# A Fourier mixing layer and a tanh-shrink feed-forward layer on one core: another order of the element-wise steps, of the transforms' banks and of the second layer's products

## The chip, the cores and the metric

The kernel runs on one core of a Trainium2 chip. A core has a matrix engine (TensorE, PE in the profile), two engines for element-wise work that can read the matrix engine's output memory (VectorE, DVE, and ScalarE, ACT), a third for element-wise work[...] (GpSimd, POOL), and DMA queues. Each engine works through its own instructions in the order in which the program lists them, and engines wait for each other at semaphores. Matmul results go to PSUM[...]; a bank here is one tile of 128 partitions by 512 fp32 values.

The metric is the time of one execution on the device, in microseconds.

## The reference

```python
# x (8, 3008, 256), filters (1505, 256), w_in (256, 2048), w_out (2048, 256), all fp32
X = np.fft.rfft(x, axis=1)
Y = X * (filt_r + 1j * filt_i)[None]
y = np.fft.irfft(Y, n=3008, axis=1)
tokens = y.reshape(8 * 3008, 256)
h = tokens @ w_in
g = h - np.tanh(h)
out = g @ w_out
```

The length 3008 is split as 64 times 47. The transform is a chain of small matmuls with data laid out again through device memory in between: `first` (its results `pf`), then `middle` (a forward product `pz`, the filter, a backward product `pe`), then `last` (`pu`, which gives the tokens of one group). The batch is worked off in five units of one or two sequences: while the feed-forward layer of one unit runs, the transforms of the next are put between its matmuls, one at a time.

Both layers of the feed-forward part use a scheme in which a two-by-two block product takes seven block products instead of eight, numbered 1 to 7. Their weights and sums of weights are made at the start; the sums of the other operand are made as the kernel goes (`tu` for the tokens, `t` for the hidden values). `h - tanh(h)` is computed as h times y times a polynomial in y, with y the square of an arctangent of scaled h.

## The kernel before

The loop runs over U, from 0 to 193. A step U holds three things at different depths: `up(U)`, the first layer of 512 of the 2048 hidden columns for a group of up to 512 tokens; `shrink(U - 1)`, the element-wise function of the step before; `down(U - 2)`, its second layer. Four U (u = 0 to 3) make one group. `up` is the frame, and calls the next piece of `shrink` (`s`), the next piece of `down` (`d` and `e`) and a possible transform (`t(0)` to `t(4)`) at fixed places:

```python
    def up(U, d, e, s, t):
        i, u = divmod(U, 4)
        b, tu, w = uts[i]
        rhs = [b[0][0], b[1][0], b[1][1], tu[:, 3, 0:w], tu[:, 0, 0:w], tu[:, 1, 0:w],
               tu[:, 2, 0:w]]
        banks = {k: ps.tile([128, 2, 256], F32, tag=k, bufs=1, name=k) for k in "xyz"}
        X, Y, Z = (banks[k][:, :, 0:w] for k in "xyz")
        h = dn.tile([128, 4, 2, 256], F32, tag="h", bufs=3, name="h")
        hs[U] = (h, w)
        def mm(bank, q, first):
            for k in range(2):
                nc.tensor.matmul(bank[:, k], wu[:, q - 1, (2 * u + k) * 128:(2 * u + k + 1) * 128],
                                 rhs[q - 1], start=(first and k == 0), stop=True,
                                 skip_group_check=True)
        def copied(tag):
            t = dn.tile([128, 2, 256], F32, tag=tag, bufs=1, name=tag)[:, :, 0:w]
            ACT.copy(t, X)
            return t
        steps_at = ([1, 2, 0, 1, 0, 1, 1, 0] if U > 1 else [0, 0, 1, 0, 2, 0, 1, 2])
        def shrinks(at):
            for _ in range(steps_at[at]):
                s()
        mm(X, 1, True)
        mm(Y, 2, True)
        s1 = copied("s1")
        t(0)
        d()
        shrinks(0)
        V.tensor_add(h[:, 0, :, 0:w], Y, s1)
        e()
        shrinks(1)
        t(1)
        mm(X, 6, False)
        mm(Z, 5, True)
        u2 = copied("u2")
        shrinks(2)
        d()
        shrinks(3)
        e()
        t(2)
        mm(X, 7, False)
        u3 = copied("u3")
        V.tensor_add(h[:, 3, :, 0:w], Z, u3)
        shrinks(4)
        d()
        shrinks(5)
        e()
        t(3)
        mm(X, 4, False)
        V.tensor_copy(h[:, 2, :, 0:w], X)
        shrinks(6)
        d()
        e()
        t(4)
        mm(Z, 3, False)
        V.tensor_add(h[:, 1, :, 0:w], Z, u2)
        shrinks(7)
    def shrink(U):
        h, w = hs.pop(U)
        ht = {k: h[:, k:k + 2].rearrange("p a b n -> p (a b) n")[:, :, 0:w] for k in (0, 2)}

```

X, Y and Z are three PSUM banks with one tile each. X and Z take several products one after another: they are read out in between, and the next product adds to what is there. `h[:, 0]` to `h[:, 3]` are the four blocks of hidden values.

The element-wise function of a step comes in six pieces; half 2 is h2 and h3, half 0 is h0 and h1. `combine` makes the four sums of blocks on GpSimd:

```python
        yield
    def combine(b, t, shared=False):
        G.tensor_sub(t[0], b[0][1], b[0][0])
        G.tensor_sub(t[1], b[1][1], t[0])
        (V if shared else G).tensor_sub(t[2], b[1][1], b[0][1])
# ...
            return dn.tile([128, 4, 256], F32, tag=tag, bufs=bufs, name=tag)[:, :, 0:w]
        y, sq = {}, {}
        def start(k):
            y[k] = tiles("y", 2)
            ACT.activation(y[k], ht[k], AF.Arctan, scale=S)
            ACT.activation(y[k], y[k], AF.Square,
                           accum_out=y_sums[:, 2 * U + k // 2:2 * U + k // 2 + 1])
        def square(k):
            sq[k] = tiles("sq", 1)
            V.tensor_mul(ht[k], ht[k], y[k])
            ACT.activation(sq[k], y[k], AF.Square, bias=near_b, scale=A)
        def end(k):
            V.scalar_tensor_tensor(out=ht[k], in0=sq[k], scalar=K, in1=ht[k],
                                   op0=ALU.add, op1=ALU.mult)
        start(2)
        yield
        square(2)
        yield
        end(2)
        yield
        start(0)
        yield
        square(0)
        yield
        end(0)
        t = dn.tile([128, 4, 2, 256], F32, tag="t", bufs=2, name="t")
        blocks = [[h[:, 2 * a + k, :, 0:w] for k in range(2)] for a in range(2)]
        combine(blocks, [t[:, k, :, 0:w] for k in range(4)], U + 1 == 4 * len(groups))
        gs[U] = (blocks, t, w)
        yield
    accs, stores, outs = {}, [], []
```

The second layer has eight pieces, called in turn by `d` and `e`. Seven sums stay in four banks over the four U of a group:

```python

        i, u = divmod(U, 4)
        b, t, w = gs.pop(U)
        rhs = [b[0][0], b[1][0], b[1][1], t[:, 3, :, 0:w], t[:, 0, :, 0:w], t[:, 1, :, 0:w],
               t[:, 2, :, 0:w]]
        if u == 0:
            accs[i] = [ps.tile([128, 2, 256], F32, tag=f"o{k}", bufs=1, name=f"o{k}")
                       for k in range(4)]
        acc = accs[i]
        at = {1: (0, 0), 2: (0, 1), 3: (1, 0), 5: (1, 1), 6: (2, 0), 7: (2, 1), 4: (3, 0)}
        def product(q):
            bank, k = at[q]
            return acc[bank][:, k, 0:w]
        def mm(*qs):
            for k in range(2):
                for q in qs:
                    nc.tensor.matmul(product(q), wd[:, q - 1, (2 * u + k) * 128:
                                                    (2 * u + k + 1) * 128],
                                     rhs[q - 1][:, k], start=(u == 0 and k == 0 and q == qs[0]),
                                     stop=(u == 3 and k == 1), skip_group_check=True)
        done = u == 3
        if done:
            p1, p5, u2, x12 = (dn.tile([128, 256], F32, tag=k, bufs=1, name=k)[:, 0:w]
                               for k in ("p1", "p5", "pu2", "x12"))
            o = dn.tile([128, 2, CH * 128], F32, tag="o", bufs=1, name="o")
        mm(1, 2)
        yield
        if done:
            ACT.copy(p1, product(1))
            V.tensor_add(o[:, 0, 0:w], product(2), p1)
        yield
        mm(3, 5)
        yield
        if done:
            ACT.copy(p5, product(5))
            V.tensor_add(x12, product(3), p5)
        yield
        mm(6, 7)
        yield
        if done:
            V.tensor_add(u2, product(6), p1)
            V.tensor_add(p1, product(7), u2)
            G.tensor_add(o[:, 0, w:2 * w], u2, x12)
        yield
        mm(4)
        yield
        if done:
            V.tensor_add(o[:, 1, 0:w], product(4), p1)
            G.tensor_add(o[:, 1, w:2 * w], p1, p5)
            accs.pop(i)
            if i + 1 < len(groups):
                stores.append((i, o))
            else:
                store_last(i, o)
        yield
    def store(i, o):

```

A transform asks for a bank with `zd`; `quarter` is the place, 0 to 4, at which `t` was called, and `latest` the bank of the last transform. There are two banks for it, t (its own) and y (the same bank as Y above):

```python
            quarter, latest = [1], ["t"]
            def zd(name, shape):
                latest[0] = "y" if quarter[0] in (1, 2, 3) and latest[0] == "t" else "t"
                return ps.tile(shape, F32, tag=latest[0], bufs=1, name=name)
```

One step of `middle` is a `pz` with its filter, the next one a `pe` of the `pz` before:

```python
        def back():
            j, uv = waiting.pop(0)
            pe = z("pe", [128, per, w])
            for i in range(per):
                k = per * j + i
                nc.tensor.matmul(pe[0:RP2, i], mats[k // 4][1][:, k % 4], uv[0:IM + RP, i],
                                 start=True, stop=True)
            e1 = tr.tile([RP2, 2, DM], F32, tag="e1", bufs=2, name="e1")
# ...
            pz = z("pz", [128, per, w])
            at, ft = a2[j // 2] if j % 2 == 0 else a2.pop(j // 2)
            for i in range(per):
                k = per * j + i
                lo = j % 2 * BD + i * w
                nc.tensor.matmul(pz[:, i], mats[k // 4][0][0:R2, k % 4],
                                 at[0:R2, lo:lo + w], start=True, stop=True)
            uv = tr.tile([128, per, w], F32, tag="uv", bufs=2, name="uv")
            zs = tr.tile([128, per, w], F32, tag="zs", bufs=2, name="zs")
            lo = j % 2 * per
            fr, fi = (ft[:, v, lo:lo + per, :] for v in range(2))
            if pair:
                fr, fi = (f.to_broadcast([128, 2, DM]) for f in (fr, fi))
            def rows(t):
                return t.rearrange("p i (b c) -> p (i b) c", c=DM)
            ACT.mul(zs[0:IM], pz[IM:128], -1.0)
            ACT.copy(zs[IM:128], pz[0:IM])
            V.tensor_mul(rows(uv), rows(pz), fr)
            G.tensor_mul(rows(zs), rows(zs), fi)
            G.tensor_add(uv, uv, zs)
            waiting.append((j, uv))
            yield
            if len(waiting) > 1:
                back()
                yield
        back()
```

Which transform is called, if any, follows from the step's number: at quarters 0 and 2 of u = 3 it is always a `pu`; elsewhere the pieces of `first` and then of `middle` are spread over the unit's steps.

Of the kernel before, what the change touches and what calls it, by code (L numbers as in the profile page):

```python
# [9 lines left out]
F32 = mybir.dt.float32  # L10
# [133 lines left out]
def kernel(  # L144
# [10 lines left out]
    V, G, ACT = nc.vector, nc.gpsimd, nc.scalar  # L155
# [376 lines left out]
    def up(U, d, e, s, t):  # L532

        i, u = divmod(U, 4)
        b, tu, w = uts[i]
        rhs = [b[0][0], b[1][0], b[1][1], tu[:, 3, 0:w], tu[:, 0, 0:w], tu[:, 1, 0:w],
               tu[:, 2, 0:w]]
        banks = {k: ps.tile([128, 2, 256], F32, tag=k, bufs=1, name=k) for k in "xyz"}
        X, Y, Z = (banks[k][:, :, 0:w] for k in "xyz")
        h = dn.tile([128, 4, 2, 256], F32, tag="h", bufs=3, name="h")  # L540
        hs[U] = (h, w)

# [11 lines that stand above are left out]

        steps_at = ([1, 2, 0, 1, 0, 1, 1, 0] if U > 1 else [0, 0, 1, 0, 2, 0, 1, 2])

        def shrinks(at):
            for _ in range(steps_at[at]):  # L560
# [10 lines that stand above are left out]
        shrinks(1)  # L571
        t(1)
        mm(X, 6, False)
        mm(Z, 5, True)
        u2 = copied("u2")
        shrinks(2)
# [8 lines that stand above are left out]
        d()  # L585
        shrinks(5)
        e()
        t(3)
        mm(X, 4, False)
        V.tensor_copy(h[:, 2, :, 0:w], X)  # L590
        shrinks(6)
        d()
        e()
# [10 lines that stand above are left out]
        def tiles(tag, bufs):  # L604
            return dn.tile([128, 4, 256], F32, tag=tag, bufs=bufs, name=tag)[:, :, 0:w]

        y, sq = {}, {}

        def start(k):
            y[k] = tiles("y", 2)  # L610
            ACT.activation(y[k], ht[k], AF.Arctan, scale=S)  # L611
            ACT.activation(y[k], y[k], AF.Square,  # L612
                           accum_out=y_sums[:, 2 * U + k // 2:2 * U + k // 2 + 1])

        def square(k):
            sq[k] = tiles("sq", 1)
            V.tensor_mul(ht[k], ht[k], y[k])  # L617
            ACT.activation(sq[k], y[k], AF.Square, bias=near_b, scale=A)  # L618

        def end(k):  # L620
            V.scalar_tensor_tensor(out=ht[k], in0=sq[k], scalar=K, in1=ht[k],  # L621
                                   op0=ALU.add, op1=ALU.mult)

        start(2)
        yield
        square(2)
        yield
        end(2)
        yield
        start(0)  # L630
        yield
        square(0)
        yield
        end(0)
        t = dn.tile([128, 4, 2, 256], F32, tag="t", bufs=2, name="t")
        blocks = [[h[:, 2 * a + k, :, 0:w] for k in range(2)] for a in range(2)]
# [3 lines that stand above are left out]
# [3 lines left out]
    def down(U):  # L643
# [18 lines that stand above are left out]
                for q in qs:  # L662
                    nc.tensor.matmul(product(q), wd[:, q - 1, (2 * u + k) * 128:  # L663
                                                    (2 * u + k + 1) * 128],
                                     rhs[q - 1][:, k], start=(u == 0 and k == 0 and q == qs[0]),
                                     stop=(u == 3 and k == 1), skip_group_check=True)

        done = u == 3
        if done:
            p1, p5, u2, x12 = (dn.tile([128, 256], F32, tag=k, bufs=1, name=k)[:, 0:w]  # L670
                               for k in ("p1", "p5", "pu2", "x12"))
            o = dn.tile([128, 2, CH * 128], F32, tag="o", bufs=1, name="o")
        mm(1, 2)
        yield
        if done:
            ACT.copy(p1, product(1))
            V.tensor_add(o[:, 0, 0:w], product(2), p1)
        yield
        mm(3, 5)
        yield  # L680
        if done:
            ACT.copy(p5, product(5))
            V.tensor_add(x12, product(3), p5)
        yield
# [18 lines that stand above are left out]
# [136 lines left out]
    with tc.tile_pool(name="tr", bufs=2) as tr, tc.manual_schedule():  # L839
        with tc.tile_pool(name="pro", bufs=1) as pro, \  # L840
                tc.tile_pool(name="ps0", bufs=6, space=bass.MemoryType.PSUM) as ps0:

            def z0(name, shape):
                return ps0.tile(shape, F32, tag="z", bufs=6, name=name)
# [132 lines left out]
            for j in range(NK // 2):  # L977
# [6 lines left out]
                pz = z0("pz", [128, 2, DM])  # L984
                for i in range(2):
                    k = (2 * j + i) % 4
# [34 lines left out]
        with tc.tile_pool(name="dn", bufs=2) as dn, \  # L1021
                tc.tile_pool(name="ps", bufs=1, space=bass.MemoryType.PSUM) as ps:

            quarter, latest = [1], ["t"]

            def zd(name, shape):
                latest[0] = "y" if quarter[0] in (1, 2, 3) and latest[0] == "t" else "t"
                return ps.tile(shape, F32, tag=latest[0], bufs=1, name=name)  # L1030

            psums.append(zd)
# [37 lines left out]
            for U in range(total + 2):  # L1070
                i, u = divmod(U, 4)
                if U < total:
                    p, c = groups[i]
                    if c == 0 and u == 0:
                        units = 4 * len(CHUNKS[p])
                        steps, done = [], 0 if p else EARLY
# [21 lines left out]
                def d():  # L1098

                    next(dw, None)  # L1100

                def e():

                    next(dw, None)

                def s():

                    next(sh, None)

                def t(k):  # L1110


                    nonlocal ms, done
                    quarter[0] = k
                    if k == 2 and stores:
                        store(*stores.pop())
                    store_some(4)
                    if U >= total:
                        return
                    pos = 20 * c + 5 * u + k  # L1120
                    if u == 3 and k in (0, 2) and i + 1 < len(groups):
                        next(lasts)
                    elif done < len(steps) and steps[done] <= pos:
                        if done < n_f:
                            next(fs)
                        else:
                            next(ms)
                        done += 1
                        if done == n_f:
                            ms = middle(p + 1, z1)  # L1130
                            next(ms)
                    next(late, None)
                    if U > 0 and k in (1, 3):
                        next(copies, None)
# [56 lines left out]
```

## Time and profile before

| What | Value |
|---|---|
| Time, median of 3 runs | 2817.25 us (2815.6 to 2819.74) |
| Span of the profiled execution | 2817.1 us |
| TensorE busy | 2725.6 us, 12438 matmul instructions |
| VectorE busy | 1913.8 us |
| ScalarE busy | 1877.0 us |
| GpSimd busy | 1796.2 us |
| DMA | 217.53 MB, 77 GB/s in the mean |

A row of the profile's groups names the line, the engine, the operation and the tiles (out<-in), the number of instructions, their busy time and the mean duration of one in ns. A row of the waits reads: engine, tile and line that waited, whom it waited for, microseconds in total, number of times, longest. A row of the timeline reads: start in us, duration in us, engine, line, operation, tiles, number of instructions merged into it, and in brackets the idle time before it with its releaser. PE is a matmul, PEld a weight load. Recorded ends of matmuls lie behind the start of the next one, since they are pipelined. One matmul of the program is two matmul instructions in the trace, so a group of two calls on 256 columns shows as x4.

Lines of the kernel before: L545 first layer, L551 copies out of X, L569, L583, L590 and L596 the VectorE readings of Y, Z, X and Z that give h0, h3, h2 and h1; L611 arctangent, L612 its square, L618 square with bias, L617 product, L621 end of the element-wise function; L524 to L527 the sums on GpSimd; L663 second layer; L430, L411, L351 and L511 `pz`, `pe`, `pf` and `pu`; L443 and L444 ScalarE's two readings of `pz`, L445 VectorE's, L446 and L447 GpSimd's part of the filter.

### The profile page before, as it was taken

Reading aid. Unit: us, or ns where it says so; the run is one execution under the profiler, and the core shown is the slowest. Engines: PE = TensorE matmul, PEld = TensorE weight load, DVE = VectorE, ACT = ScalarE, POOL = GpSimd, SP = SyncE. Lnnn points to the kernel's source line nnn. Section 1 sums busy time; section 2 is a strip of 40 time slices with the busy share of each in tenths; the row PEclk is TensorE's granted clock in tenths of the full one; section 3 lists DMA queues with packets and bytes.
Section 4 is the critical chain, followed back from the end, with each engine's and each line's share of the span. In section 5 each row is a group of like instructions: output and inputs, shape, how many; then the busy total and the mean of one; then the engine's idle time right before and its main releaser. Section 6 shows DMA issues by size and latency. Waiting matters only on the chain.

```text
span 2817.1 us, 36653 instructions
## 1 busy us (share of the span) xinstructions
PE 2725.6 (97%) x12438; PEld 2268.1 (81%) x12438; DVE 1913.8 (68%) x2175; ACT 1877.0 (67%) x2790; POOL 1796.2 (64%) x1407
## 2 busy tenths in 40 slices
PE   4899999999999999999999999999999999999998
PEld 2577777888878777888878887888888888898887
DVE  6755666666766676666677767666676777677776
ACT  2466776666667766666667776666666676666665
POOL 5546887544776767644576777755476666655555
PEclk7999999999999999999999999999999999999999
DMA  9854443332333322223323233112223322101010
GB/s 248 220 180 118 104 123 76 87 87 72 72 77 79 74 68 61 58 81 83 88 70 76 68 79 81 40 41 67 58 65 64 77 56 57 30 19 26 16 23 17
DMA packets 322592, 217.53 MB, mean 77 GB/s; under 512 B 224782, under 2 KB 274746, under 8 KB 322156
## 3 DMA queue, kind: packets, MB, share of 16 engines
q1 hardware_dynamic: 266826, 157.28, 24.0%
q10 hardware_dynamic: 52818, 51.53, 6.0%
q0 software_dynamic: 2752, 6.30, 0.8%
q8 instruction: 100, 1.64, 0.3%
q14 instruction: 96, 0.79, 0.1%
HBM read 138.87 MB, written 79.17 MB: 77 GB/s over the span
## 4 chain that ended last, share of the span: by engine, by line
PE 79%; ACT 8%; DVE 4%; issue 4%; DMA 3%; POOL 2%; ACTq 0%; SPq 0%; DVEq 0%; POOLq 0%
PE o L663 32%; PE x L545 20%; PE z L545 9%; PE y L545 5%; PE pe L411 3%; PE pu L511 3%; PE pz L430 3%; ACT y L611 2%; PE pf L351 2%; ACT u L551 1%; DVE h L617 1%; ACT zs L444 1%; ACT zs L443 1%; ACT y L612 1%; DVE h L590 1%
## 5 line engine op out<-in xcount | busy, mean ns | idle before, releaser
L663 PE MATMUL o<-t,wd 128*128 128x256 f32 (+2 forms) x3072 | 776.0, 375 | 1.8 <-POOL t L526 1.3
L617 DVE TENSOR_TENSOR h<-h,y 128x1024 f32<-128x1024 f32 (+2 forms) x384 | 572.4, 1491 | 275.8 <-ACT y L612 275.8
L663 PEld LDWEIGHTS o<-t,wd 128*128 128x128 f32 x3072 | 580.4, 190 | 74.1 <-POOL t L526 1.6
L545 PE MATMUL x<-tu,wu 128*128 128x256 f32 (+2 forms) x2304 | 587.6, 377 | 10.8 <-ACT u L551 10.5
L663 PE MATMUL o<-h,wd 128*128 128x256 f32 (+2 forms) x2304 | 582.3, 375 | 0.4 <-DVE h L621 0.4
L621 DVE SCALAR_TENSOR_TENSOR h<-sq,h 128x1024 f32<-128x1024 f32 (+2 forms) x384 | 567.5, 1478 | 20.6 <-ACT y L611 0.5
L524 POOL TENSOR_TENSOR t<-h 128x512 f32<-128x512 f32 (+2 forms) x192 | 240.1, 1250 | 503.7 <-DVE h L621 451.9
L545 PEld LDWEIGHTS x<-tu,wu 128*128 128x128 f32 x2304 | 426.3, 190 | 154.0 <-issue 68.9
L663 PEld LDWEIGHTS o<-h,wd 128*128 128x128 f32 x2304 | 431.1, 190 | 71.9 <-issue 18.4
L618 ACT ACTIVATE sq<-y,near_b 128x1024 f32<-128x1024 f32 (+2 forms) x384 | 435.6, 1134 | 5.0 <-DVE h L621 0.2
L611 ACT ACTIVATE y<-h 128x1024 f32<-128x1024 f32 (+2 forms) x384 | 400.0, 1042 | 15.7 <-ACT e L414 8.0
L612 ACT ACTIVATE y<-y 128x1024 f32<-128x1024 f32 (+2 forms) x384 | 399.2, 1040 | 12.2
L551 ACT COPY s<-x 128x512 f32<-128x512 f32 (+2 forms) x192 | 110.7, 577 | 441.6 <-PE x L545 433.0
L527 POOL TENSOR_TENSOR t<-t,h 128x512 f32<-128x512 f32 (+2 forms) x192 | 309.2, 1610 | 0.1
L551 ACT COPY u<-x 128x512 f32<-128x512 f32 (+2 forms) x384 | 218.9, 570 | 56.8 <-PE x L545 20.3
L525 POOL TENSOR_TENSOR t<-h,t 128x512 f32<-128x512 f32 (+2 forms) x192 | 240.8, 1254 | 15.1
L583 DVE TENSOR_TENSOR h<-z,u 128x512 f32<-128x512 f32 (+2 forms) x192 | 129.5, 674 | 176.8 <-ACT u L551 173.9
L526 POOL TENSOR_TENSOR t<-h 128x512 f32<-128x512 f32 (+2 forms) x191 | 248.0, 1298 | 0.0
L446 POOL TENSOR_TENSOR zs<-zs,ft 128x512 f32<-128x512 f32 x112 | 168.6, 1505 | 91.8 <-ACT zs L444 91.7
L447 POOL TENSOR_TENSOR uv<-uv,zs 128x512 f32<-128x512 f32 x112 | 210.7, 1881 | 15.6 <-DVE uv L445 7.2
L545 PE MATMUL x<-ut,wu 128*128 128x256 f32 (+2 forms) x768 | 198.7, 381 | 8.4 <-DVE h L590 4.8
L569 DVE TENSOR_TENSOR h<-y,s 128x512 f32<-128x512 f32 (+2 forms) x192 | 130.3, 679 | 102.0 <-PE y L545 89.1
(122 smaller groups left out, 3383.7 us busy)
## 6 DMA issues: line engine op xcount, KB each, us to landing
a<-ct SPq DMA_DIRECT2D x64, 384.0 KB, 4.0
ft<-filt SPq DMA_DIRECT2D x96, 256.0 KB, 4.7
out_dram<-ot SPq DMA_DIRECT2D x1392, 16.0 KB, 1.5
ct<-e ACTq DMA_DIRECT2D x112, 192.0 KB, 2.3
ct<-a ACTq DMA_DIRECT2D x80, 256.0 KB, 2.9
x_sb<-in_x_dram SPq DMA_DIRECT2D x69, 256.0 KB, 2.8
e<-ct SPq DMA_DIRECT2D x33, 512.0 KB, 4.5
fg<-fg SPq DMA_DIRECT2D x40, 392.0 KB, 6.2
```

The source lines that it names most:

```text
L524: G.tensor_sub(t[0], b[0][1], b[0][0])
L525: G.tensor_sub(t[1], b[1][1], t[0])
L526: (V if shared else G).tensor_sub(t[2], b[1][1], b[0][1])
L527: G.tensor_sub(t[3], t[1], b[1][0])
L545: nc.tensor.matmul(bank[:, k], wu[:, q - 1, (2 * u + k) * 128:(2 * u + k + 1) * 128], rhs[q - 1], start=(first and k == 0), stop=True, ski ...
L551: ACT.copy(t, X)
L611: ACT.activation(y[k], ht[k], AF.Arctan, scale=S)
L612: ACT.activation(y[k], y[k], AF.Square, accum_out=y_sums[:, 2 * U + k // 2:2 * U + k // 2 + 1])
L617: V.tensor_mul(ht[k], ht[k], y[k])
L618: ACT.activation(sq[k], y[k], AF.Square, bias=near_b, scale=A)
L621: V.scalar_tensor_tensor(out=ht[k], in0=sq[k], scalar=K, in1=ht[k], op0=ALU.add, op1=ALU.mult)
L663: nc.tensor.matmul(product(q), wd[:, q - 1, (2 * u + k) * 128: (2 * u + k + 1) * 128], rhs[q - 1][:, k], start=(u == 0 and k == 0 and q == ...
```

## The change

Four things change together. The six pieces of the element-wise function are cut anew and called at other places: the square with bias of half 2 comes behind the copy u2, the square (`power`) and the square with bias of half 0 behind the copy u3. The product of half 0 comes behind the copy of h2 out of X, and the transform of quarter 3 behind that copy as well. Z is given out only where its first product comes, so that a transform at quarter 0, if it isn't a `pz`, may use Z's bank between two steps. The second layer takes its products in the order 2, 3, 1, 5, 6, 7, 4, with the start flag on the first product of each bank in that order. The aim is to let the copies that free the PSUM banks come early in their engines' queues. No instruction is added or taken away, and no shape changes.

```diff
--- before.py
+++ after.py
@@ -535,8 +535,11 @@
         b, tu, w = uts[i]
         rhs = [b[0][0], b[1][0], b[1][1], tu[:, 3, 0:w], tu[:, 0, 0:w], tu[:, 1, 0:w],
                tu[:, 2, 0:w]]
-        banks = {k: ps.tile([128, 2, 256], F32, tag=k, bufs=1, name=k) for k in "xyz"}
-        X, Y, Z = (banks[k][:, :, 0:w] for k in "xyz")
+
+        def bank(k):
+            return ps.tile([128, 2, 256], F32, tag=k, bufs=1, name=k)[:, :, 0:w]
+
+        X, Y = bank("x"), bank("y")
         h = dn.tile([128, 4, 2, 256], F32, tag="h", bufs=3, name="h")
         hs[U] = (h, w)
 
@@ -554,7 +557,7 @@
 
 
 
-        steps_at = ([1, 2, 0, 1, 0, 1, 1, 0] if U > 1 else [0, 0, 1, 0, 2, 0, 1, 2])
+        steps_at = ([1, 1, 1, 1, 0, 1, 1, 0] if U > 1 else [0, 0, 1, 0, 2, 0, 2, 1])
 
         def shrinks(at):
             for _ in range(steps_at[at]):
@@ -571,6 +574,7 @@
         shrinks(1)
         t(1)
         mm(X, 6, False)
+        Z = bank("z")
         mm(Z, 5, True)
         u2 = copied("u2")
         shrinks(2)
@@ -585,9 +589,9 @@
         d()
         shrinks(5)
         e()
-        t(3)
         mm(X, 4, False)
         V.tensor_copy(h[:, 2, :, 0:w], X)
+        t(3)
         shrinks(6)
         d()
         e()
@@ -606,31 +610,40 @@
 
         y, sq = {}, {}
 
-        def start(k):
+        def turn(k):
             y[k] = tiles("y", 2)
             ACT.activation(y[k], ht[k], AF.Arctan, scale=S)
+
+        def power(k):
             ACT.activation(y[k], y[k], AF.Square,
                            accum_out=y_sums[:, 2 * U + k // 2:2 * U + k // 2 + 1])
 
+        def times(k):
+            V.tensor_mul(ht[k], ht[k], y[k])
+
         def square(k):
             sq[k] = tiles("sq", 1)
-            V.tensor_mul(ht[k], ht[k], y[k])
             ACT.activation(sq[k], y[k], AF.Square, bias=near_b, scale=A)
 
         def end(k):
             V.scalar_tensor_tensor(out=ht[k], in0=sq[k], scalar=K, in1=ht[k],
                                    op0=ALU.add, op1=ALU.mult)
 
-        start(2)
+
+        turn(2)
+        power(2)
+        yield
+        times(2)
         yield
         square(2)
+        turn(0)
         yield
         end(2)
         yield
-        start(0)
-        yield
+        power(0)
         square(0)
         yield
+        times(0)
         end(0)
         t = dn.tile([128, 4, 2, 256], F32, tag="t", bufs=2, name="t")
         blocks = [[h[:, 2 * a + k, :, 0:w] for k in range(2)] for a in range(2)]
@@ -662,7 +675,8 @@
                 for q in qs:
                     nc.tensor.matmul(product(q), wd[:, q - 1, (2 * u + k) * 128:
                                                     (2 * u + k + 1) * 128],
-                                     rhs[q - 1][:, k], start=(u == 0 and k == 0 and q == qs[0]),
+                                     rhs[q - 1][:, k],
+                                     start=(u == 0 and k == 0 and q in (2, 3, 6, 4)),
                                      stop=(u == 3 and k == 1), skip_group_check=True)
 
         done = u == 3
@@ -670,15 +684,14 @@
             p1, p5, u2, x12 = (dn.tile([128, 256], F32, tag=k, bufs=1, name=k)[:, 0:w]
                                for k in ("p1", "p5", "pu2", "x12"))
             o = dn.tile([128, 2, CH * 128], F32, tag="o", bufs=1, name="o")
-        mm(1, 2)
+        mm(2, 3)
+        yield
+        yield
+        mm(1, 5)
         yield
         if done:
             ACT.copy(p1, product(1))
             V.tensor_add(o[:, 0, 0:w], product(2), p1)
-        yield
-        mm(3, 5)
-        yield
-        if done:
             ACT.copy(p5, product(5))
             V.tensor_add(x12, product(3), p5)
         yield
@@ -1023,10 +1036,12 @@
 
 
 
+
             quarter, latest = [1], ["t"]
 
             def zd(name, shape):
-                latest[0] = "y" if quarter[0] in (1, 2, 3) and latest[0] == "t" else "t"
+                other = "tyyyt"[quarter[0]] if quarter[0] or name == "pz" else "z"
+                latest[0] = other if latest[0] == "t" else "t"
                 return ps.tile(shape, F32, tag=latest[0], bufs=1, name=name)
 
             psums.append(zd)
```

## The prediction

> **What bounds the kernel now.** I read the page first, then the stretches, the list of waits, and at the end single stretches of the timeline, engine by engine.
>
> ```profile
> span 2817.1 us, 36653 instructions
> ...
> PE 2725.6 (97%) x12438; PEld 2268.1 (81%) x12438; DVE 1913.8 (68%) x2175; ACT 1877.0 (67%) x2790; POOL 1796.2 (64%) x1407
> ...
> PE  4899999999999999999999999999999999999998
> ```
>
> TensorE is busy almost everywhere outside the first 150 us and at a full granted clock (1.00 in every stretch from 150 to 2780 us), so the change can only win idle time of TensorE, and the busy share hides how much that is, because the recorded ends of matmuls overlap. I therefore use starts: eight matmuls of 256 columns take 1.73 us from the first start to the next group's start, so one costs 0.216 us, a group of four 0.86 us. Adding up every start-to-start distance between 200 and 2790 us of the timeline and taking off the full-speed time by the columns (2538.2 of 2589.9 us) leaves **51.8 us of gaps**. That is the ceiling of any gain in the loop: 1.8% of the span. They fall into few kinds:
> - 14.0 us in 37 gaps between a second-layer matmul and a group on X with `tu` (the 7th or 4th product), and 11.2 us in 39 gaps between the last group on Z and the next unit's first group on X;
> - about 8 us because the matmul after each of these 76 gaps is also 0.104 us slow;
> - 12.3 us ahead of `pe` transforms (one of 3.0 us, seven of 1.2 us in the dense stretch 281 to 453 us), the rest scattered.
>
> The waits name the releasers of the first two kinds:
>
> ```profile
> DVE uv L445 <- ACT zs L444: 112.5, 76, 3.2
> ...
> PEld x L545 <- ACT u L551: 34.5, 73, 1.9
> ...
> PEld x L545 <- DVE h L590: 24.1, 49, 2.2
> ...
> PE x L545 <- ACT u L551: 10.5, 26, 1.1
> ```
>
> X is one PSUM bank: each group that adds to it waits until ScalarE has copied the sum out (L551), and a new unit waits until VectorE has (L590). Before those copies stand other things in the same engine's queue. One unit in full, first TensorE, then VectorE:
>
> ```profile
> 1602.46 1.02 PE L430 MATMUL pz<-a,fg 94*128 94x512 f32 x2
> 1603.32 1.03 PE L545 MATMUL x<-tu,wu 128*128 128x256 f32 x4
> 1604.19 1.03 PE L663 MATMUL o<-t,wd 128*128 128x256 f32 x4
> 1605.05 1.03 PE L545 MATMUL z<-ut,wu 128*128 128x256 f32 x4
> 1606.20 1.13 PE L545 MATMUL x<-ut,wu 128*128 128x256 f32 x4
> 1607.16 1.03 PE L545 MATMUL y<-ut,wu 128*128 128x256 f32 x4
> 1608.03 1.02 PE L411 MATMUL pe<-uv,fg 112*96 112x512 f32 x2
> ```
>
> ```profile
> 1604.85 0.69 DVE L445 TENSOR_TENSOR uv<-pz,ft 128x512 f32<-128x512 f32 x1 [0.61 <-ACT zs L444]
> 1605.46 0.68 DVE L590 COPY h<-x 128x512 f32<-128x512 f32 x1
> 1606.06 1.21 DVE L621 SCALAR_TENSOR_TENSOR h<-sq,h 128x1024 f32<-128x1024 f32 x1
> 1607.19 0.41 DVE L695 TENSOR_TENSOR o<-o,p 128x256 f32<-128x256 f32 x1
> 1607.53 0.68 DVE L596 TENSOR_TENSOR h<-z,u 128x512 f32<-128x512 f32 x1
> 1608.33 0.69 DVE L569 TENSOR_TENSOR h<-y,s 128x512 f32<-128x512 f32 x1
> ```
>
> The copy of X stands behind `uv`, which waits for ScalarE's two `zs` copies of the `pz` at quarter 3; so X is free at 1606.14 and the next unit starts at 1606.20 instead of 1605.91. Note for later where Z comes free: at 1608.21 (1607.53 + 0.68). Nothing on TensorE asks for it at 1608.03, since `pe` goes to bank t.
>
> [...] a copy whose data are ready waits behind `uv`. [...] `uv` waits for `zs` 76 times, 112.5 us. [...] the product at L617 takes 1.21 us at 1602.23, 2.19 us at 1612.34 beside a GpSimd subtraction, 1.49 us in the mean. [...]
>
> **What it removes.** (a) The copy of h2 out of X comes ahead of the quarter-3 transform and of the product of h0. X is readable about 1.07 us after its group starts (2601.56 to ScalarE's copy at 2602.63), the copy takes 0.68, so X is free 1.75 us after its last group starts, and the next unit asks at the earliest 2.6 us after (three groups). All 39 gaps go: 11.2 + 39 x 0.104 = 15 us. (b) ScalarE's order: the square with bias (1.15 us) moves behind the copy u2, and power of h0 (1.06 + 0.19 us) behind u3; each copy can come over 1 us earlier. The 37 gaps are at most 0.87 us: 14.0 + 37 x 0.104 = 18 us. (c) Second layer: 2 and 3 read only h2 and h3, finished half a unit earlier; 1 and 5 come 2.6 us later than 1 did. That buys what the later h0 needs, and nothing by itself. Sum: **-33 us**, perhaps 3 more before 200 us and in the dense stretch.
>
> **What it adds.** The product and the end of h0 now both stand behind the copy of h2 and, in a unit with a quarter-3 transform, behind its `uv`; the addition that frees Z (L596) stands behind them. And Z is now asked for at quarter 0. From the program's step rule I list the bank of every transform: 57 use Z, all at quarter 0. With s the start of the unit's last X group:
> - `pz` at quarter 3, none at quarter 4 (14 cases: 10 `pe`, 4 `pu`). TensorE: X, pz, product 4, Z, X, Y, so it asks at s + 6 x 0.86 = s + 5.2. VectorE: `pz` readable s + 1.93, two `zs` to s + 3.1, `uv` starts 3.2, product 3.8, end 4.95, addition 6.1 to 6.8. Wait 1.6 us; GpSimd's product on `zs` starts with `uv` and takes 1.27 us[...]: I take 2.2 us. 14 x 2.2 = 31 us. In the unit above: product behind `uv` from 1605.5 or so, Z free near 1610, `pe` wanted at 1607.6.
> - neither quarter used (17 cases): copy s + 1.07, product 1.7, end 2.85, addition 4.0 to 4.7; TensorE asks at s + 4.3. 17 x 0.4 = 7 us, among them the last stage, whose last-of-four units now take 13.87 us with no gap.
> - the other 26: 0 to 0.3 us, 3 us in all.
> - a `pe` at quarter 4 in bank t right behind a `pz` at quarter 3 that is now also in t (6 units of the dense stretch; it was in y): asked at s + 2.6, `uv` done at s + 3.95: 6 x 1.35 = 8 us.
> - Y is freed later too, about 3 us.
>
> Sum +52 us. Net +52 - 33 - 3 = +16 us, 2833. Some of it overlaps: a stall gives ScalarE and GpSimd time to catch up, which other gaps don't then need, so I take **2828 us** (+0.4%).
>
> **Rivals.** *The gaps go and nothing takes their place*: then about 2780. For it: the copies are the named releasers. Against it: Z was never waited for at quarter 0 before, as t held those transforms, and the six-group count above is tight. *It stays level*: [...]the z waits are smaller, because ScalarE reaches `zs` early; with 1.2 us in the first case and half of the others the sum is +28 and the time about 2809. *The late h0 reaches the second layer*: GpSimd's first difference then ends near s + 8 to 9.3, and product 5 is wanted at s + 8.6 where no stall precedes; then the stall sits there as well, in up to 17 units, some 10 us more: 2843. VectorE as a bound is ruled out: 68% busy, and no instruction is added.
>
> **Range and chances.** All rivals lie between 2780 and 2843; the middle is 2828, and I give 2798 to 2850. Faster by over 2% needs 56 us, more than all gaps of the loop: 0.02. Slower by over 2% needs 56 us net, twice what I add: 0.05. Within 2%: 0.93.
>
> **What would show it.** Right: `PE x` behind `DVE h` (copy of h2) and behind `ACT u` nearly gone from the waits; new waits of `PE pe` and `PE pu` for the addition that frees Z, 1.5 us or more behind a `pz` at quarter 3; the last stage's last-of-four units near 14.3 us. Wrong: quarter-0 transforms start 0.86 us after Y throughout; or the waits of X persist, meaning that ScalarE, not the order, was late.

## The result, and the profile after

| Kernel | Median (lowest to highest) | Ratio to before, 95% interval | Mean granted clock, profiled run |
|---|---|---|---|
| before | 2817.25 us (2815.6 to 2819.74) | | 0.991 |
| after | 2903.41 us (2899.79 to 2905.17) | 1.0301 [1.0287, 1.0316] | 0.982 |

The change makes the kernel 86 us slower. The range on record ended at 2850 us, 53 us short of that.

Line numbers have moved: L548 is now the first layer, L554 ScalarE's copies, L593 the copy of h2, L600 the addition that frees Z, L622 the product and L629 the end of the element-wise function, L676 the second layer. L445 to L447, the filter, have kept theirs. From the head of the page of after:

```profile
PE 2745.7 (95%) x12438; PEld 2286.2 (79%) x12438; DVE 1913.8 (66%) x2175; ACT 1886.6 (65%) x2790; POOL 1782.8 (61%) x1407
```

TensorE has the same 12438 matmuls, but 20 us more busy time (2725.6 before). So two things have grown: its idle time, and the time of some matmuls. The list of waits of after (engine and line that waits, what it waited for: us in total, times, longest) names the idle part:

```profile
PE pe L411 <- DVE h L600: 34.9, 17, 3.5
...
PE pu L511 <- DVE h L600: 19.5, 17, 3.1
...
PE x L548 <- ACT u L554: 3.5, 4, 1.9
```

Neither of the first two is in the list of before: they are transforms that now go to Z's bank and wait for the addition that reads it. The last line is the old wait for X, 10.5 us in 26 cases before. The wait of X for VectorE's copy has gone altogether.

The same step as in the prediction, in the timeline of after; TensorE first:

```profile
1654.72 1.03 PE L548 MATMUL x<-tu,wu 128*128 128x256 f32 x4
...
1659.04 1.03 PE L548 MATMUL y<-ut,wu 128*128 128x256 f32 x4
1663.60 1.07 PE L411 MATMUL pe<-uv,fg 112*96 112x512 f32 x2 [3.53 <-DVE h L600]
1664.50 3.10 PE L676 MATMUL o<-h,wd 128*128 128x256 f32 x8
```

and VectorE:

```profile
1657.98 0.69 DVE L445 TENSOR_TENSOR uv<-pz,ft 128x512 f32<-128x512 f32 x1 [1.50 <-ACT zs L444]
1658.59 1.73 DVE L622 TENSOR_TENSOR h<-h,y 128x1024 f32<-128x1024 f32 x1
1660.35 2.17 DVE L629 SCALAR_TENSOR_TENSOR h<-sq,h 128x1024 f32<-128x1024 f32 x1
...
1662.78 0.68 DVE L600 TENSOR_TENSOR h<-z,u 128x512 f32<-128x512 f32 x1
```

and GpSimd, beside the product and the end:

```profile
1657.96 1.27 POOL L446 TENSOR_TENSOR zs<-zs,ft 128x512 f32<-128x512 f32 x1 [1.81 <-ACT zs L444]
1659.31 2.12 POOL L447 TENSOR_TENSOR uv<-uv,zs 128x512 f32<-128x512 f32 x1
```

The next step's X groups now follow without a gap, and then `pe` stands 3.53 us: `uv`, product, end and the addition follow each other on VectorE, and only the last one frees Z. Then comes what the prediction had no term for: the eight matmuls after `pe` take 3.10 us; before they took 1.89. Two stretches of TensorE behind the stall show why (length, busy time, matmuls, granted clock, DMA share, GB/s):

```profile
1666.00:1668.00 2.00, 2.00 (x6) 0.50 0.79 247
...
1670.00:1672.00 2.00, 2.00 (x11) 1.00 0.00 0
```

After the stall the clock is granted at half for some 3 us (0.76 in the stretch from 1664, 0.50 from 1666, 0.89 from 1668, 1.00 from 1670). I add up, as in the prediction, the distances between matmul starts beyond full speed ("extra distance" below); from 200 us to where the last stage ends (2790 us before, about 2870 after) they are 52 us before and 134 us after. By the lengths of steps U = 0 to 190, each from its first group on X to the next step's, after minus before; the first three rows are cases of the prediction, and a wait for Z at quarter 0 counts in the step in which it falls:

| Steps | Number | After minus before |
|---|---|---|
| Z wanted behind a `pz` at quarter 3 | 14 | +62.4 us |
| neither quarter 3 nor 4 used | 17 | +9.0 us |
| dense stretch, `pe` at quarter 4 behind `pz`, both in t | 6 | +10.3 us |
| behind a step with a `pz` at quarter 3, no transform at quarter 0 | 8 | +16.5 us |
| all others | 146 | -14.5 us |

The sum is 83.7 us; the rest lies ahead of and behind these steps.

### The profile page after: what moved, and what is told of

It reads as the page before. It is cut to its first block, busy times and chain, and to the rows that moved or that the text cites. A ratio compares the mean times of both kernels' runs of the same rounds, so it can differ in the third digit from the quotient of the medians.

```text
span 2899.7 us, 36331 instructions
## 1 busy us (share of the span) xinstructions
PE 2745.7 (95%) x12438; PEld 2286.2 (79%) x12438; DVE 1913.8 (66%) x2175; ACT 1886.6 (65%) x2790; POOL 1782.8 (61%) x1407
## 4 chain that ended last, share of the span: by engine, by line
PE 78%; DVE 9%; POOL 4%; ACT 3%; issue 3%; DMA 2%; ACTq 0%; SPq 0%; DVEq 0%; POOLq 0%
PE o L676 34%; PE x L548 19%; PE z L548 9%; PE y L548 4%; PE pe L411 4%; PE pu L511 3%; PE pz L430 3%; DVE h L622 2%; PE pf L351 2%; DVE h L629 2%; DVE uv L445 1%; POOL t L526 1%; DVE h L600 1%; ACT zs L444 1%; POOL t L527 1%
## 5 line engine op out<-in xcount | busy, mean ns | idle before, releaser
L622 DVE TENSOR_TENSOR h<-h,y 128x1024 f32<-128x1024 f32 (+2 forms) x384 | 565.2, 1472 | 350.3 <-ACT y L618 350.2
L676 PE MATMUL o<-t,wd 128*128 128x256 f32 (+2 forms) x3072 | 776.3, 375 | 5.4 <-POOL t L526 3.6
L629 DVE SCALAR_TENSOR_TENSOR h<-sq,h 128x1024 f32<-128x1024 f32 (+2 forms) x384 | 563.3, 1467 | 172.3 <-ACT sq L626 149.2
L676 PEld LDWEIGHTS o<-t,wd 128*128 128x128 f32 x3072 | 578.6, 190 | 107.0 <-issue 29.3
L524 POOL TENSOR_TENSOR t<-h 128x512 f32<-128x512 f32 (+2 forms) x192 | 240.9, 1255 | 681.5 <-DVE h L629 603.1
L676 PE MATMUL o<-h,wd 128*128 128x256 f32 (+2 forms) x2304 | 596.1, 382 | 0.0
L548 PE MATMUL x<-tu,wu 128*128 128x256 f32 (+2 forms) x2304 | 585.8, 377 | 3.5 <-ACT u L554 3.5
L548 PEld LDWEIGHTS x<-tu,wu 128*128 128x128 f32 x2304 | 433.4, 191 | 106.9 <-issue 44.2
L676 PEld LDWEIGHTS o<-h,wd 128*128 128x128 f32 x2304 | 441.3, 195 | 77.7 <-issue 24.6
L626 ACT ACTIVATE sq<-y,near_b 128x1024 f32<-128x1024 f32 (+2 forms) x384 | 434.9, 1132 | 7.6 <-DVE h L629 1.4
L554 ACT COPY u<-x 128x512 f32<-128x512 f32 (+2 forms) x384 | 221.1, 576 | 154.6 <-PE x L548 137.6
L527 POOL TENSOR_TENSOR t<-t,h 128x512 f32<-128x512 f32 (+2 forms) x192 | 319.3, 1663 | 0.1
L554 ACT COPY s<-x 128x512 f32<-128x512 f32 (+2 forms) x192 | 110.9, 578 | 311.2 <-PE x L548 293.1
L526 POOL TENSOR_TENSOR t<-h 128x512 f32<-128x512 f32 (+2 forms) x191 | 288.6, 1511 | 0.0
L525 POOL TENSOR_TENSOR t<-h,t 128x512 f32<-128x512 f32 (+2 forms) x192 | 250.6, 1305 | 15.1
L593 DVE COPY h<-x 128x512 f32<-128x512 f32 (+2 forms) x192 | 130.3, 679 | 139.8 <-PE x L548 139.5
L447 POOL TENSOR_TENSOR uv<-uv,zs 128x512 f32<-128x512 f32 x112 | 199.8, 1783 | 9.0 <-DVE uv L445 0.2
L548 PE MATMUL z<-tu,wu 128*128 128x256 f32 (+2 forms) x768 | 196.0, 378 | 1.9 <-DVE h L600 1.9
```

Of the source, the lines that this page charges most:

```text
L527: G.tensor_sub(t[3], t[1], b[1][0])
```

## The experiments

The theory after this reading: asking for Z at quarter 0 while its last reader stands behind `uv`, product and end is the cause, and the half clock after a stall makes it dearer. The rivals: the new order of steps is itself the cause; the second layer's order is; or waits for GpSimd are. Theory C of the expectations is that the longer product and end are all of it: beside GpSimd's two filter operations they took 1.73 and 2.17 us above, where the prediction counted about 1.14 each. "The lock" is the author's name for this lengthening; by what means one engine delays the other, no run shows. Times are medians, ratios are to the kernel before.

### Old banks in the new order

```diff
-                other = "tyyyt"[quarter[0]] if quarter[0] or name == "pz" else "z"
-                latest[0] = other if latest[0] == "t" else "t"
+                latest[0] = "y" if quarter[0] in (1, 2, 3) and latest[0] == "t" else "t"
```

> The changed kernel, but transforms use banks t and y alone, by the rule of before. Theory A (TensorE stalls because it asks for Z at quarter 0 while Z still waits behind uv, product and end of h0): all 57 quarter-0 requests for Z vanish, with them 62 us in the 14 steps behind a pz at quarter 3, 9 us in the 17 steps without transforms at quarters 3 and 4, 10 us in the dense stretch; the gaps on X stay away. 2790 to 2815 us. Theory B (the late h0 itself holds up the second layer, and Z is only where the delay shows): the wait moves to the second layer's first use of h0 and of the first difference, time stays above 2870 us.

Measured: 2811.72 us, ratio 0.9974 [0.9963, 0.9985]: 92 us less than after, and slightly better than before. By cases the 14 steps are at -0.1 us, the 17 at -4.4, the dense stretch at -0.2, the 8 at +9.1. VectorE frees Z just as late as in after. In a step whose last X group starts at 1612.71, its timeline has

```profile
1620.43 0.68 DVE L600 TENSOR_TENSOR h<-z,u 128x512 f32<-128x512 f32 x1
```

but TensorE's goes on at once, since `pu` is in bank t:

```profile
1617.37 1.03 PE L548 MATMUL y<-ut,wu 128*128 128x256 f32 x4
1618.23 1.05 PE L511 MATMUL pu<-s_sb,e 128*128 128x128 f32 x8
```

So the late addition costs little by itself (about 3 us in eight places where Z's own next product waits for it); it costs when a transform asks for its bank. The opposite run follows.

### Z's bank in the old order

The kernel before with the change's `zd`, and Z's tile made just ahead of its first product:

```diff
-        banks = {k: ps.tile([128, 2, 256], F32, tag=k, bufs=1, name=k) for k in "xyz"}
+        X, Y = bank("x"), bank("y")
...
+        Z = bank("z")
         mm(Z, 5, True)
...
-                latest[0] = "y" if quarter[0] in (1, 2, 3) and latest[0] == "t" else "t"
+                other = "tyyyt"[quarter[0]] if quarter[0] or name == "pz" else "z"
+                latest[0] = other if latest[0] == "t" else "t"
```

> The kernel before, with Z's bank for transforms at quarter 0 as the only part of the change. Theory A: in the order of before, end of h0 and the addition that frees Z come early (Z free at about the time at which the quarter-0 transform asks, 0 to 0.6 us late), so 2817 to 2835 us: the bank alone does little, the harm needs the late h0 as well. If asking for Z were harmful in itself: 2880 us or more.

Measured: 2829.51 us, ratio 1.0034 [1.0021, 1.0047]. The 14 steps are only 2.1 us longer; the dense stretch is 8.3 us longer here too, so that most of that term belongs to the banks alone. Z's bank alone costs 12 us, the new order with the old banks gains 6; together they cost 86. It is the combination.

### Product and end ahead of the quarter-3 transform

```diff
         V.tensor_copy(h[:, 2, :, 0:w], X)
-        t(3)
         shrinks(6)
+        t(3)
```

> The changed kernel, with product, end and differences of half 0 placed ahead of the quarter-3 transform instead of behind it, so that they no longer stand behind uv. Theory A: Z comes free about 4.7 us after the last X group starts and is asked for at 5.2 us, so the 14 long stalls nearly vanish and no half clock follows them; also the 8 stalls on Y behind a pz at quarter 3; 2815 to 2835 us. If the lock between VectorE and GpSimd alone makes the stall (theory C), the order against uv matters little and the time stays above 2870 us.

Measured: 2857.24 us, ratio 1.013 [1.0113, 1.0146]; more than expected. The 14 steps fell from +62.4 to +1.2 us, so their stalls are settled by the place in VectorE's queue. But now the filter stands behind the product and the end, and on GpSimd behind the four sums. `pe` waits for it, for the filter's result (L447) or for VectorE's reading of `pz` that frees bank t (L445). From this kernel's list of waits:

```profile
PE pe L411 <- POOL uv L447: 18.8, 6, 5.5
...
PE pe L411 <- DVE uv L445: 13.5, 6, 2.3
```

The dense stretch went from +10.3 to +19.1 us, by the second of these waits. Of the 8 steps behind a `pz` at quarter 3 six lost their excess, as expected, but the two where a `pe` was called at quarter 4 are 8.7 and 7.2 us longer than before, by the first. Whichever of the two comes first on VectorE, the other is late.

### GpSimd's part of the filter later

This takes GpSimd's two filter operations away from beside the product and the end, to test how much of the stall comes from product and end being longer there. `rest` holds the two:

```diff
             V.tensor_mul(rows(uv), rows(pz), fr)
-            G.tensor_mul(rows(zs), rows(zs), fi)
-            G.tensor_add(uv, uv, zs)
             waiting.append((j, uv))
             yield
+            rest()
```

> The changed kernel, with GpSimd's two filter operations (product on zs, sum into uv) put off to the next transform step, so that they no longer run beside product and end of h0. Theory A with the lock as a part: product and end take 1.2 us each instead of 1.7 and 2.2, the stall at Z falls from 3.5 to about 2 us[...]; 2840 to 2865 us. Theory C (the lock is all of it): close to 2825 us. If the lock matters nothing: 2900 us.

Measured: 2926.72 us, ratio 1.0382 [1.0365, 1.04], and so far above what was expected, since the filter's result (L449 here) is now late for `pe`, mostly in the dense stretch. In the list of waits:

```profile
PE pe L411 <- POOL uv L449: 60.0, 11, 7.7
```

The total says nothing on the question, but the 14 steps do: +27.2 us instead of +62.4. In one of them VectorE's timeline is (L626 the product, L633 the end)

```profile
1548.70 1.22 DVE L626 TENSOR_TENSOR h<-h,y 128x1024 f32<-128x1024 f32 x1
1549.95 1.22 DVE L633 SCALAR_TENSOR_TENSOR h<-sq,h 128x1024 f32<-128x1024 f32 x1
```

2.4 us for the two instead of 3.9. TensorE in that step, and in another where the wait was longer (L604 the addition that frees Z, L680 the second layer):

```profile
1551.92 1.07 PE L411 MATMUL pe<-uv,fg 112*96 112x512 f32 x2 [1.74 <-DVE h L604]
1552.83 1.89 PE L680 MATMUL o<-h,wd 128*128 128x256 f32 x8
...
1698.94 1.23 PE L411 MATMUL pe<-uv,fg 112*96 112x512 f32 x2 [2.07 <-DVE h L604]
1699.97 3.46 PE L680 MATMUL o<-h,wd 128*128 128x256 f32 x8
```

A wait of 1.74 us is followed by a full-speed group (granted clock 1.00 from 1552 to 1556), one of 2.07 us by half the clock (0.50 from 1701 to 1703). In the 14 steps the stalls fall from 47.4 to 27.5 us of extra distance, 1.4 us each; ten lose the half clock with it, four keep it.

### Unread matmuls in the stall

Seven matmuls whose result nobody reads, in bank t, ahead of each of the 14 requests for Z. They leave the wait as it is and only keep TensorE busy during it (`now` is the place 5U + k of the call, `before_it` the place and name of the last transform; the lines that keep them are left out here and below):

```diff
                 latest[0] = other if latest[0] == "t" else "t"
+                if latest[0] == "z" and before_it[0] == (now[0] - 2, "pz"):
+                    fill = ps.tile([128, 2, 128], F32, tag="t", bufs=1, name="fill")
+                    for _ in range(7):
+                        nc.tensor.matmul(fill, wf1[:, 0], wf1, start=True, stop=True)
```

> The changed kernel, with seven matmuls that nobody reads put into bank t ahead of the transform in each of the 14 steps where it asks for Z behind a pz at quarter 3: 3.0 us of work inside a stall of 3.1 to 3.5 us, so the stall ends when it did, but TensorE isn't idle in it. Theory D (the idle time itself costs more, because the granted clock falls to 0.5 for about 3 us after it): the eight second-layer matmuls behind the stall take 1.7 us again instead of 2.9 to 3.4; 14 times 1.2 to 1.7 us, so 2879 to 2887 us. If the slow matmuls have another cause (their data late, GpSimd): 2903 us or a little more.

Measured: 2879.06 us, ratio 1.0225 [1.0208, 1.0242]. More work, about 24 us less time. TensorE's timeline at one of the 14:

```profile
1683.58 1.03 PE L548 MATMUL y<-ut,wu 128*128 128x256 f32 x4
1684.44 3.18 PE L1049 MATMUL fill<-wf_sb 128*128 128x256 f32 x14
1687.72 1.10 PE L411 MATMUL pe<-uv,fg 112*96 112x512 f32 x2
1688.65 1.89 PE L676 MATMUL o<-h,wd 128*128 128x256 f32 x8
```

The wait is there still (`pe` starts 4.14 us after the Y group instead of 0.86), but the group behind takes 1.89 us. The 14 steps fell from +62.4 to +40.7: the half clock is 21.7 us of theirs. The timeline of after agrees: the slow matmuls behind its 14 stalls add up to 22.7 us.

### The second layer's order, without it and alone

The kernel with old banks, with the second layer back in the order 1, 2, 3, 5, 6, 7, 4; and the kernel before with the new order only. The first, in short (the second is its reverse):

```diff
-        mm(2, 3)
-        yield
-        yield
-        mm(1, 5)
+        mm(1, 2)
...
+        mm(3, 5)
```

> The changed kernel with banks t and y alone, and the second layer in its old order 1, 2, 3, 5, 6, 7, 4. If the new order only makes room for the late h0, product 1 now waits for it in every step with a pz at quarter 3 (asked for at about 5.2 us after the last X group starts, h0 finished near 8): 2 to 3 us and then half clock in some 30 steps, 2870 us or more. If h0 isn't that late: 2812 us.

> The kernel before with the new order of the second layer as the only part of the change. There h0 and its sums are finished in time for either order, so no gap of TensorE should come or go: 2815 to 2820 us. A clear difference would mean that the order itself (banks of the sums, weights) costs or brings something.

Measured: the first 2853.57 us, ratio 1.0134 [1.0117, 1.0151], 42 us more than with the new order, though less than expected (the waits are 1.4 us in the mean, and slow matmuls follow only four of them); the second 2817.58 us, ratio 1.0001 [0.9992, 1.001]. The waits of the first show what the order is for:

```profile
PE o L676 <- DVE h L629: 53.0, 37, 2.5
```

Product 1 waits for the late end of h0. With the new order this line is absent. The order carries the late h0, and buys nothing by itself.

### A version that keeps what helps

First, on the old banks, a transform at quarter 1 goes to bank t when the transform before it is at least three places back; this was to take away a wait for Y that was supposed in the 8 steps:

```diff
-                latest[0] = "y" if quarter[0] in (1, 2, 3) and latest[0] == "t" else "t"
+                far = quarter[0] == 1 and now[0] - before_it[0][0] > 2
+                latest[0] = ("y" if quarter[0] in (1, 2, 3) and latest[0] == "t" and not far
+                             else "t")
```

> The changed kernel with banks t and y alone as in the run with the old banks, and besides t instead of y at quarter 1 wherever the last transform lies three or more places back. Theory A (what is left there are waits for the late reading of Y, behind the same late h0): the 9 us that the 8 steps without a transform at quarter 0 behind a pz at quarter 3 lost go, 2798 to 2806 us. If they come from elsewhere: 2812 us.

Measured: 2809.22 us, ratio 0.9967 [0.9956, 0.9977]. The 8 steps are still at +8.1 us. But by the step rule the new bank falls into only one of them; there a wait of 1.99 us for VectorE's reading of Y gave way to one of 1.02 us for GpSimd's third sum, and the step became 0.9 us shorter. So the run does not test Y in the other seven. With the old banks five of these wait for that sum, or on Z for the late addition, two 0.24 us each for Y. Next the product of h0 goes back ahead of the copy of h2, with all else kept:

```diff
         power(0)
+        times(0)
         square(0)
         yield
-        times(0)
         end(0)
```

> The kernel of the run with bank t at quarter 1, with the product of h0 ahead of the copy of h2 again (as in the kernel before), everything else kept. The product is then done before the last X group ends in most steps, and h0 is finished 1.1 to 1.7 us earlier. If what is left of waits in that kernel comes from the late h0 (theory A): 2798 to 2806 us. If the copy of h2 then stands in the queue long enough to hold up X again, the gain is given back: 2809 to 2815 us.

Measured: 2806.32 us (2804.59 to 2806.98), ratio 0.9949 [0.9931, 0.9967], the lowest median of all, though its interval overlaps those of the kernel with old banks and of the one with bank t at quarter 1. It lies just above the first range expected. The 8 steps are at +0.8 us: the late h0 was the reason of what was left there. For it 38 gaps between Z and the next X are back, 15.6 us of extra distance. Last, the same with the quarter-3 transform ahead of the last X group again:

```diff
+        t(3)
         mm(X, 4, False)
         V.tensor_copy(h[:, 2, :, 0:w], X)
-        t(3)
```

> As the run with the product first, and the transform of quarter 3 ahead of the last X group again as well, so that of the four moves only the two squares on ScalarE and the order of the second layer are left. The gaps between Z and the next step's X (11 us in 39 places before) should be back, the gaps behind ScalarE's copies stay away: 2800 to 2808 us. If the ScalarE order alone is what brings the gain, this is as fast as the run with the product first or faster.

Measured: 2814.49 us, ratio 0.9986 [0.9975, 0.9996]. The gaps between Z and the next X are now 61, with 23.7 us, more than in before. The transform's move behind the copy is worth 8 us; most of the gain of the version ahead of this one hangs on it, and the order on ScalarE with that of the second layer brings some 3 us.

## Why the prediction was wrong, point by point

**Removing the gaps of X (-33 us): right in kind, too high in worth.** The gaps between the second layer and X went from 14.0 to 1.7 us of extra distance, those between Z and X from 11.2 to 0, the slow matmuls inside X groups from 10.0 to 2.8: 30.7 us together. But the steps that have no new wait became only 14.5 us shorter. The kernel with old banks shows why, as no transform waits for Z there: the extra distance ahead of `pe` behind a second-layer matmul rose from 12.3 to 25.9 us (15 of these 21 waits end with VectorE's reading of Y, six with the filter), that within the second layer, for GpSimd's sums, by about 6 us, and the whole gained 6 us. What the shorter X wait gave, the later h0 took back, since the reading of Y and the sums stand behind it. The prediction had the sums as a rival of 10 us and Y as a term of 3.

**"14 x 2.2 = 31 us": the step that failed.** The cases, the time at which Z is asked for and the start of the chain were right: in the step above, with s = 1654.72, `pe` was due at s + 5.2 and the product began at s + 3.9, against 5.2 and 3.8 predicted. Mis-sized were the two operations behind `uv`: 1.14 us or so each, plus the 0.6 that was added to the wait for GpSimd's product (2.2 us taken instead of 1.6), makes 2.9; they took 1.73 + 2.17 = 3.9 us. The 0.6 was put on one operation and both became longer, as GpSimd's product (from 1657.96) is followed at once by its addition (from 1659.31). The late filter shows it: without these neighbours 1.22 + 1.22. In four of the 14 a reading of the second layer's sums (L708 in this step) stands ahead of the addition as well. So TensorE lost 47.4 us in the 14 cases (3.27 to 3.70 each, 3.38 in the mean) instead of 31.

**The term that was missing: the clock.** The prediction read a full clock in every stretch and took it as given. Its stretches were hundreds of us long. The one wait of 3.0 us that it lists shows the drop already in before, in a stretch of 2 us:

```profile
244.66 1.15 PE L411 MATMUL pe<-uv,fg 112*96 112x512 f32 x2 [2.87 <-POOL uv L447]
```

```profile
246.00:248.00 2.00, 2.00 (x6) 0.50 1.09 247
```

The slow matmuls behind it lost 1.75 us. The filled stalls put the half clock at 21.7 us in the 14 steps of after; of the 24 us in the whole, some 3 come from two stalls that were not filled and kept the full clock this time. 47.4 + 21.7 is 69.1; the 62.4 measured is less, by what these steps gained at X.

**The smaller terms.** Neither quarter used: 7 us predicted, 9.0 measured, and the last stage's last-of-four steps take 14.7 us, where 14.3 was said. The other 26: 3 predicted, about 0 measured. The dense stretch: 8 predicted, 10.3 measured; the bank change alone gives 8.3. "Y is freed later too, about 3 us" was right in kind and too small, and it is not all of the 16.5 us in the eight steps. In four of them `pe` asks for bank y and waits 1.5 to 2.1 us (shown as idle); they hold 10.7 us, 3.4 of which is half clock behind two waits of 2.09 us. At these two the profile names a sum on GpSimd (L524), but that ends after `pe` has started (1114.52); VectorE's reading of Y ends 0.14 us ahead of it, as the addition does at Z:

```profile
1113.70 0.68 DVE L572 TENSOR_TENSOR h<-y,s 128x512 f32<-128x512 f32 x1
```

The other four steps hold 5.9 us, waits for GpSimd's third sum and of Z's own next product for the late addition. The first are of the kind of the third rival, the second was not on the list.

**The sum.** Added 98 us instead of 52 (62.4 + 9.0 + 10.3 + 16.5, and nothing for the 26), removed 14.5 instead of 36 (33 and the 3 more). Of the 68 us between the net of +16 and the 84 of these steps, the 14 cases make 31, the shortfall at X 21.5, the eight steps 13.5. The argument against 56 us net was that it needed "twice what I add". That treated the estimate as its own upper bound: no rival made the central wait longer than the 2.2 us taken.

**Left open.** Whether a place for Z's addition exists that frees it in time and keeps the gaps of X closed wasn't tried. Nor was the half clock separated from the waits in the 17 steps, where none was seen.

## What to carry to other kernels

Before a bank gets a second user, find its last reader in that engine's queue and add up what stands ahead of it, each operation at the length it has beside its actual neighbours on GpSimd, not at its mean (here 1.73 and 2.17 us for two operations that took 1.22 each without them). Count a TensorE stall of 2 us or more as possibly longer than itself (slow matmuls followed 46 of the 58 waits from 2.07 us on that are counted below), look at the granted clock in stretches as short as the stall, and let an upper case of the range hold that. Where the profile names what ended a wait, see that it really ended before the wait did.

## What the runs showed of the hardware that was not expected

Behind a stall, TensorE's granted clock can fall to half (0.50 from 1666 to 1668 in after), and how often depends on the length. Between 200 us and the last step, over the traces of all twelve kernels, slow matmuls followed none of 32 waits shown as 1.5 to 2.0 us idle, 8 of 14 at 2.07 to 2.30, 4 of 6 at 2.46 to 2.53, 1 of 3 at 2.87 to 2.89, 8 of 10 at 3.11 to 3.12 and all 25 from 3.44 us on. (The extra distance between starts is 0.16 us more.) In the 12 of the 14 stalls of after that were followed by slow matmuls, 1.6 to 2.9 us were lost behind each, the transform included.

The same wait can go either way. In after the matmuls behind one of 2.09 us are slow (granted clock 0.50 from 1116 to 1118):

```profile
1114.52 1.07 PE L411 MATMUL pe<-uv,fg 112*96 112x512 f32 x2 [2.09 <-POOL t L524]
1115.43 1.85 PE L548 MATMUL x<-tu,wu 128*128 128x256 f32 x4
```

and in the kernel with filled stalls, at the same place of the program, they are not (1.00 from 1113 to 1117):

```profile
1112.02 1.07 PE L411 MATMUL pe<-uv,fg 112*96 112x512 f32 x2 [2.09 <-POOL t L524]
1112.92 1.03 PE L548 MATMUL x<-tu,wu 128*128 128x256 f32 x4
```

What decides between the two, no run here shows.
